# Leaving the sums of two spectral weight products to the inverse transform's matmuls

## The chip, the cores and the metric

The kernel runs on one core of one Trainium2 chip. The metric is the device time of one execution in microseconds (us), given as the median over several runs. A difference under 2% gets the verdict "same", so the 95% interval of each ratio is given too.

## The reference

Two equal layers are applied to a sequence of 2048 rows of 448 elements in bf16. Each is a spectral layer (normalise, two-dimensional real FFT, multiply by a complex weight, inverse FFT, add) followed by a dense layer (normalise, matmul to 1792, squared relu, matmul back, add).

```python
def _A_ref(x, w_r, w_i):
    X = jnp.fft.rfft2(x.astype(jnp.float32), axes=(-2, -1))
    X = X * (w_r + 1j * w_i)
    return jnp.fft.irfft2(X, s=(S, D), axes=(-2, -1)).astype(jnp.bfloat16)

def _B_ref(x, w1, b1, w2, b2):
    h = jnp.einsum("bsd,df->bsf", x, w1) + b1
    h = jnp.where(h > 0, h, 0) ** 2
    return jnp.einsum("bsf,fd->bsd", h, w2) + b2

x = A_x
for _ in range(2):                      # written out twice in the reference
    x = x + _A_ref(_layernorm(x), A_w_r, A_w_i)
    x = x + _B_ref(_layernorm(x), B_w1, B_b1, B_w2, B_b2)
```

What matters is `X * W`. A complex product is four real products, one sum and one difference: Re = Xr·Wr − Xi·Wi, Im = Xr·Wi + Xi·Wr.

## The kernel before

The spectral stage works through nine groups of frequencies, numbered 0 to 8. Seven of them are pairs (p = 2, 3 up to 14, 15). Each group passes through these units: TD (forward transform along the rows, matmuls on TQ), an eviction, B (forward transform along the sequence, matmuls on G), an eviction, W (the products with the weights, on VectorE, into `tmp`), Ws (their sum and difference, on VectorE, into `Z`, which lies in the buffer called `arena`), Bi (inverse transform along the sequence, matmuls whose moving operand is the table H and whose stationary operand comes from `Z`), and an eviction into `VT`. The stage TI then transforms back along the rows.

```python
GROUPS = ((1,), (2, 3), (4, 5), (6, 7), (8, 9), (10, 11), (12, 13), (14, 15), (0,))

def stage_W(ps_, slot):
    ...
    for f, W in enumerate((Wa, Wb)):              # products with w_r, then with w_i
        ...
        tt(... T[:, f], X, a, ALU.mult)           # T is a part of tmp
    if p == 0:
        return
    z = z.rearrange("p q f l -> p f q l")
    rank("Ws")
    for i, op in enumerate((ALU.add, ALU.subtract)):   # the sums
        tt(z[:, 2 * i:2 * i + 2], T[:, :, :, 0], T[:, :, ::-1, 1], op)

def stage_Bi(p, slot):
    ...
    for lb in range(2):
        ...
        plan = [(o(0, None), 2, h(0)), (o(1, None), 0, h(64)), (o(0, None), 3, h(192)), (o(1, None), 1, h(256))]
        for n, (out_, i, w) in enumerate(plan):    # 8 matmuls for one p
            mm(out_, Z[:, slot, i, lb:2 * P:2], w, ...)   # 128 columns, step 2
    evac(VT[...], ps[...], "Bie")
```

A list scheduler within the kernel orders all these units on the engines. Its inputs are the tables PR (a priority for each unit) and EN (which engine may take each eviction). Where TensorE would otherwise be idle, the scheduler inserts "fillers": matmuls of 512 columns on a tile of ones whose result nobody reads, meant to keep the engine's activity up:

```python
def warm_mm(b):
    return lambda e: e.matmul(ps[:, b, :], ones[:], ones[:, None, :].to_broadcast([P, 4, P]), start=True, stop=True)
```

The dense layer that follows needs its input transposed. For some of the rows a transposing DMA does this (`yT<-xin`), and the matmuls on `yT` wait for its landing.

## Time and profile before

| | |
|---|---|
| time before (3 runs) | 265.75 us (265.22 to 265.8) |
| span of the profiled run | 264.1 us |
| stage that changes | 142.82 to 164.35 us (21.53 us) |

Here are three lines of the kernel before: from its page, the busy time of each engine (us, share of the span, number of instructions) and the chain that ended last, by engine; and from busy time by stretch, exactly the stage that changes (length, then PE, PEld, DVE, ACT, POOL, each with its count, then granted clock, DMA share and GB/s):

```profile
PE 255.7 (97%) x2383; PEld 163.3 (62%) x2383; DVE 204.3 (77%) x708; ACT 183.8 (70%) x391; POOL 9.5 (4%) x21
PE 82%; DVE 7%; ACT 7%; DMA 2%; issue 1%; POOL 0%; POOLq 0%; DVEq 0%
142.82:164.35 21.53, 20.50 (x270) 17.42 (x271) 19.97 (x38) 19.23 (x30) 0.00 (x0) 1.00 0.01 2
```

PE is TensorE, PEld its weight loads, DVE VectorE and ACT ScalarE. In the stage three engines are nearly full at once.

### The profile page before, as it was taken

The page shows a single profiled execution, that of the slowest core. Times are in us where ns is not written, and L with a number is a line of the kernel's source. Part 1 is how long each engine was busy: PE and PEld are TensorE (multiplying, and loading weights), DVE is VectorE, ACT ScalarE, POOL GpSimd, SP SyncE. Part 2 cuts the span into 40 slices and gives each one's busy share as a digit, 9 for nine tenths or more (in the row PEclk, how much of TensorE's full clock was granted, in tenths as well). Part 3 has the DMA queues.
Part 4 walks back from the last instruction along what each step waited for, and adds up shares of the span by engine and source line. Part 5 has one row for each costly group of instructions (what it writes and reads, how often), then busy time and mean ns, then how long its engine had stood idle before and what let it go on. Part 6 is the DMA issues. An engine that isn't in the chain of part 4 may idle for free.

```text
span 264.1 us, 6399 instructions
## 1 busy us (share of the span) xinstructions
PE 255.7 (97%) x2383; PEld 163.3 (62%) x2383; DVE 204.3 (77%) x708; ACT 183.8 (70%) x391; POOL 9.5 (4%) x21
## 2 busy tenths in 40 slices
PE   8999999999999999999999999998999999999996
PEld 2679978768555554445577887786754444544454
DVE  4978997999999996565797998899899755223522
ACT  6978996978786388791587996976999784005700
POOL 4720000000000000000000000000000000000000
PEclk9999999999999999999999999999999999999999
DMA  6999990026606700013000000002077000110011
GB/s 185 406 351 359 387 351 21 2 43 132 183 15 151 193 9 2 0 27 116 0 2 0 2 4 0 4 0 60 2 125 149 20 0 20 37 52 19 0 37 52
DMA packets 24474, 23.25 MB, mean 88 GB/s; under 512 B 16284, under 2 KB 20988, under 8 KB 24316
## 3 DMA queue, kind: packets, MB, share of 16 engines
q1 hardware_dynamic: 23968, 21.82, 27.9%
q0 software_dynamic: 160, 0.92, 0.8%
q8 instruction: 19, 0.31, 0.5%
q10 hardware_dynamic: 316, 0.10, 0.2%
q14 instruction: 11, 0.09, 0.1%
HBM read 15.49 MB, written 2.76 MB: 69 GB/s over the span
## 4 chain that ended last, share of the span: by engine, by line
PE 82%; DVE 7%; ACT 7%; DMA 2%; issue 1%; POOL 0%; POOLq 0%; DVEq 0%
PE ps L588 79%; ACT arena L628 3%; PE ps L1157 2%; DVE arena L646 2%; DMA yT<-xin 2%; ACT XA L628 2%; ACT tmp L628 1%; DVE tmp L646 1%; DVE x_raw L936 1%; DVE st L966 1%; ACT VT L628 1%; DVE tmp L629 0%; DVE x_raw L938 0%; DVE VT L646 0%; ACT mv L611 0%
## 5 line engine op out<-in xcount | busy, mean ns | idle before, releaser
L611 ACT ACTIVATE arena<-ps,b1T 128x512 bf16<-128x512 f32 (+1 forms) x140 | 74.0, 614 | 31.2 <-PE ps L588 31.0
L588 PE MATMUL ps<-yT,W_sb 64*128 64x512 bf16 (+1 forms) x980 | 87.1, 333 | 1.1 <-DMA yT<-xin 0.7
L588 PE MATMUL ps<-W_sb,arena 128*128 128x448 bf16 (+1 forms) x476 | 86.8, 342 | 0.0
L588 PEld LDWEIGHTS ps<-yT,W_sb 64*128 64x128 bf16 x980 | 50.3, 94 | 37.4 <-ACT arena L611 5.1
L588 PEld LDWEIGHTS ps<-W_sb,arena 128*128 128x128 bf16 x476 | 46.1, 98 | 37.8 <-DVE arena L646 0.8
L646 DVE TENSOR_TENSOR arena<-arena 128x512 bf16<-128x512 bf16 (+1 forms) x140 | 48.0, 370 | 19.1 <-ACT arena L611 18.7
L1055 DVE TENSOR_TENSOR x_raw<-ps,arena 128x448 bf16<-128x448 f32 (+1 forms) x23 | 13.4, 581 | 20.8 <-PE ps L588 20.8
L628 ACT ACTIVATE arena<-ps 128x896 bf16<-128x896 f32 (+1 forms) x32 | 26.3, 911 | 2.6 <-PE ps L588 2.6
L628 ACT ACTIVATE VT<-ps 128x512 bf16<-128x512 f32 x28 | 16.5, 699 | 2.8 <-PE ps L588 2.7
L1157 PE MATMUL ps<-ones 128*128 128x512 bf16 x54 | 16.4, 428 | 1.1 <-DVE ones L659 1.1
L588 PE MATMUL ps<-H_sb,arena 128*128 128x128 bf16 x256 | 16.8, 219 | 0.7 <-DVE arena L646 0.7
L646 DVE TENSOR_TENSOR arena<-tmp 128x896 bf16<-128x896 bf16 (+1 forms) x32 | 17.1, 590 | 0.3
L738 ACT ACTIVATE tmp<-x_raw 128x448 bf16<-128x448 bf16 x14 | 8.1, 576 | 13.3 <-DVE x_raw L1051 13.2
L628 ACT ACTIVATE XA<-ps 128x512 bf16<-128x512 f32 x28 | 15.2, 593 | 2.4 <-PE ps L588 2.4
L738 ACT ACTIVATE VT<-x_raw 128x448 bf16<-128x448 bf16 x24 | 13.8, 583 | 4.3 <-DVE x_raw L938 4.3
L588 PEld LDWEIGHTS ps<-H_sb,arena 128*128 128x128 bf16 x256 | 15.0, 98 | 2.7 <-DVE arena L646 2.5
L646 DVE TENSOR_TENSOR tmp<-VT 128x224 bf16<-128x224 bf16 (+1 forms) x56 | 16.3, 322 | 0.2
L938 DVE SCALAR_TENSOR_TENSOR x_raw<-ps,x_raw 128x448 bf16<-128x448 f32 x24 | 14.3, 621 | 0.8 <-PE ps L588 0.8
L588 PE MATMUL ps<-arena,G_sb 128*128 128x224 bf16 x128 | 14.4, 259 | 0.1
L628 ACT ACTIVATE tmp<-ps 128x896 bf16<-128x896 f32 (+1 forms) x16 | 12.7, 853 | 1.9 <-PE ps L588 1.9
L758 DVE BATCH_NORM_STATS2 st<-x_raw 128x6 f32<-128x448 bf16 (+1 forms) x19 | 10.9, 589 | 2.5 <-DMA x_raw<-in_A_x_dram 2.5
L588 PEld LDWEIGHTS ps<-arena,G_sb 128*128 128x128 bf16 x128 | 11.8, 98 | 0.7 <-ACT arena L628 0.6
(78 smaller groups left out, 263.5 us busy)
## 6 DMA issues: line engine op xcount, KB each, us to landing
W_sb<-in_B_w_dram SPq DMA_DIRECT2D x2, 896.0 KB, 12.3
out_dram<-x_raw SPq DMA_DIRECT2D x15, 112.0 KB, 1.7
W_sb<-in_B_w_dram SPq DMA_DIRECT2D x1, 1568.0 KB, 17.5
x_raw<-in_A_x_dram SPq DMA_DIRECT2D x3, 448.0 KB, 7.9
H_sb<-c_H SPq DMA_DIRECT2D x1, 1088.0 KB, 9.5
yT<-xin SPq DMA_DIRECT2D x4, 225.0 KB, 5.7
Wrev<-xin SPq DMA_DIRECT2D x2, 450.0 KB
xin<-Wrev SPq DMA_DIRECT2D x4, 225.0 KB, 3.7
```

The source lines that it names most:

```text
L588: op = sch.add("pe", lambda e: e.matmul(_res(o), lhsT, rhs, start=start, stop=stop, skip_group_check=skip), [lhsT, rhs, *also], [o], cost= ...
L611: sch.add("act", lambda e: e.activation(o, _res(i), func, **kw), rd, [o], cost=c)
L628: op = sch.add("act", lambda e: e.activation(o, _res(i), ACT.Copy) if h[0].eng == "act" else e.tensor_copy(o, _res(i)), [i], [o], cost=c[" ...
L646: sch.add(eng, lambda e: e.tensor_tensor(o, _res(a), b, op), [a, b], [o], cost=_free(o) / rate + 69.0)
L738: sch.add("act", lambda e: e.activation(o, x, ACT.Square, accum_out=sd[:, t, 1:2]), [x], [o, sd[:, t, 1:2]], cost=560.0)
L758: small(lambda e, si=si, xi=xi: e.bn_stats(si, xi), [xi], [si], _free(xi) / 0.96 + 69.0)
L936: sch.add("dve", lambda e, xx=xx, xi=xi, r=r: e.tensor_tensor(xx, _res(r), xi, ALU.add), [r, xi], [xx], cost=536.0)
L938: small(lambda e, xx=xx, xi=xi, r=r, i=i: e.scalar_tensor_tensor(out=xx, in0=_res(r), scalar=1.0, in1=xi, op0=ALU.mult, op1=ALU.add, accum ...
L966: small(lambda e, i=i: e.bn_stats(st[:, i, 0:6], x_sb[:, i, 0:D]), [x_sb[:, i, 0:D]], [st[:, i, 0:6]], 536.0)
L1055: sch.add("dve", lambda e: e.tensor_tensor(o, _res(i), xb[:, t, d0:d1], ALU.add), [i, xb[:, t, d0:d1]], [o], cost=(d1 - d0) / 0.96 + 69.0)
L1157: return lambda e: e.matmul(ps[:, b, :], ones[:], ones[:, None, :].to_broadcast([P, 4, P]), start=True, stop=True)
```

## The change

The intent is to take VectorE's sums out of the stage in which VectorE is full. For groups 5 and 7 of layer 2 the inverse matmuls read the products in `tmp` directly and add them up in the accumulator. Because an accumulator only adds, the differences need a negated copy of two blocks of H, which is appended to the table. That makes 16 matmuls for each p in place of 8.

```diff
+DIRECT = ((), (10, 14))
+HX = sorted({q for d in DIRECT for p in d for q in (p, p + 1)})
 ...
-PR = {...}
-EN = {...}
+PR = {...}    # new numbers for layer 2's TD, B, W, Bi, TDe, Be, Ws, Bie; nothing else differs
+EN = {...}    # new choices for layer 2's TDe, Be, Bie
 ...
-        H_sb = sb("H_sb", [P, 15 * HQ + 4 * P])
+        H_sb = sb("H_sb", [P, 15 * HQ + (4 + 2 * len(HX)) * P])
 ...  # make_constants: the negated tables
+                if p in HX:
+                    o = 15 * HQ + (4 + 2 * HX.index(p)) * P
+                    H[:, o:o + P] = -H[:, HQ * (p - 1):HQ * (p - 1) + P]
+                    H[:, o + P:o + 2 * P] = -H[:, HQ * (p - 1) + 192:HQ * (p - 1) + 192 + P]
 ...  # stage_W
-            if p == 0:
+            if p == 0 or direct:
                 return
 ...  # stage_Bi
+                if direct:
+                    x = 15 * HQ + (4 + 2 * HX.index(p)) * P
+                    neg = [H_sb[:, x + f * P:x + (f + 1) * P] for f in range(2)]
+                    plan = []
+                    for f in range(2):
+                        a = tmp[:, 2 * (slot // 2) + f, slot % 2, 0, lb::2]
+                        c = tmp[:, 2 * (slot // 2) + f, mate % 2, 1, lb::2]
+                        plan += [(o(0, None), a, h(192 * f)), (o(1, None), a, h(192 * f + 64)),
+                                 (o(0, None), c, neg[f]), (o(1, None), c, h(192 * f + 64))]
-                    mm(out_, Z[:, slot, i, lb:2 * P:2], w, ...)
+                    mm(out_, i if direct else Z[:, slot, i, lb:2 * P:2], w, ...)
+            m = QD if direct else P       # QD = 112: only 112 partitions are evicted
```

More of the change, by code (lines that the diff above doesn't have):

```diff
@@ L79, in make_constants @@
     G = np.zeros((P, NP + 1, 192))
-    H = np.zeros((P, 15 * HQ + 4 * P))
+    H = np.zeros((P, 15 * HQ + (4 + 2 * len(HX)) * P))
     for p in range(NP):
@@ L111, in make_constants @@
                 J=np.eye(P)[::-1])
-PR = {'TD': [[1611015, 1560745, 1571669, 1391435, 1398832, -3621416, 1374866, -3479716, 1402951], [2520683, -882130, 2513278, 1403817, -946609, -1006157, -1079382, -1083072, 1408461]], 'B': [[1578993, 1416687, 1553212, 1417621, 1401279, -3584572, -3471848, 1550869, -3659354], [2513805, -1004943, 1405526, 2514030, 1385417, -1091018, 967616, -1128168, -974908]], 'W': [[1833706, 1883605, 1713507, 1845799, 1846051, 1858785, 1847117, 1976414, 992154], [258958, 196705, -32086, -31831, 199273, -68617, -58145, -231565, -289839]], 'Bi': [[-3600236, -3636088, 1397759, -3650383, -3634765, -3649053, -3658753, -3646144, -3576979], [-1103789, 969189, -981009, 1254540, 970491, 1105225, 1552262, 1255862, 1105109]], 'ln': [[991126, 1016681, 13698, -12192, 3592, -9275, 58717, 59319, 60173], [-215928, -161644, -233516, -1278285, -1243220, -1249248, -1270637, -1075997, -1090994]], 'TI': [[4661211, 3603451, 3461865, -3320802, 3581733, -3314912, 3577378, -3303437, -3557233], [1148985, 1261825, -1055731, -1010406, -1074609, -1083367, -1026469, -1043258, -1050048]], 'AI': [[3603697, 4997207, 4997530, 4979074, 3482668, 4986081, 4943161, 4901552, 4992029], [-1080862, 1269571, 943460, -1102619, 1036527, 1203915, -1142225, 1214879, 1183541]], 'xb': [[966, 109389, -75965, -110358, -218149, -39133, -137679, -133462, -146632], [-874934, -227306, -1248899, -1550879, -1543334, -1550645, -1548009, -1575947, -1598280]], 'h': [[4994138, 5003910, 4900585, 4903100, 4901125, 4954442, 5002645], [-1085930, 1201108, 1202903, 1171062, 1082119, 1231856, 1056057]], 'o': [[5025464, 5043598, 4946662, 4825629, 4947511, 4769147, 4931712, 4939797, 4905816, 4965852, 4907640, 4758088, 4928290, 3664542, 4936102, 3571000], [1035960, 1041613, 1046935, 1054242, 1080488, 1155787, 1169102, 1155870, 1000585, 1239792, 1159813, 1159789, 1170072, 1159974, 1163403, 1047019]], 'A2': [[-34871, -450185, -573944, -145705, 153605, 80879, -602905, 81580, 79768, -84049, 81902, 81224, 99503, 452346, 464311, 452106]], 'A1': [[2017417, 2016753, 2017368, 2018568, 2015776, 2016320, 2011733, 2013388]], 'aux': [[1784077, 2030436, 1458000, -222125]], 'A1x': [[-78438, 1764055, 2017145, 1740521, 1945455, 2017149, 1733606, 2013750]], 'A1f': [[2026475, 2022846, 1700588, 1673326, 1885756, 2013682, 1843661, 1757672]], 'A1m': [[1624402, 1624407, 1618344, 1618039, 1618053, 1537576, 1602322, 1670734]], 'A1e': [[2018288, 1743124, 2013324, 2018938, 1792872, 2007452, 926476, 1834891]], 'A2f': [[-34049, -127990, -606838, -439476, -138011, 89305, -571804, 80322, 86631, 80269, 450792, 462862, 54580, 466206, 59337, 450170]], 'A2s': [[480058, 130187, 326278, 591247, -431528, 73495, -83424, -22736, -590315, -851545, -746374, -585928, -115865, -441429, 129400, 466571]], 'A2m': [[4922555, 4746350, 4716000, 4727107, 4938752, 4935914, 4721112, 4719912, 3545281, -1102588, 3449906, 3544553, -1101765, 4721131, 3545586, -1101726]], 'A2e': [[43630, 40194, -682618, -204383, 162475, -55941, 457346, -202207, 210383, 251692, -640306, -43305, -207937, 110571, 278833, 493288]], 'TDe': [[2015312, 1881608, 1834874, 1912279, 933173, 1914329, 1811666, 1807467, 2012655], [234287, 1417255, 495995, 497071, -692296, -708408, 116793, 481473, -31496]], 'Be': [[1810378, 2015630, 1839426, 1797362, 938200, 1031040, 933515, 1076416, 1026320], [-673471, -562228, -700927, 509333, -668554, 482845, -571588, -638456, -610624]], 'Ws': [[1843817, 1846443, 1875937, 2003156, 1836055, 1861290, 2004506, 1857296, 1821747], [212971, -52164, -46639, -245211, -58995, -232137, -245502, -184844, -32998]], 'Bie': [[1820631, 1817640, 1818170, 1921951, 1076577, 1873067, 1921957, 1027958, 1022790], [1425225, 487576, -647465, -980124, -655085, -74395, -74265, -181695, -980116]], 'TIe': [[913909, 919877, 722393, -268012, 716509, -288603, 853646, 1008636, 792915], [-149289, -168051, -87569, -1092127, -1364282, -1052619, -148265, -1019412, -75009]], 'AIf': [[-308433, 3579, -182406, 12653, 80551, 7729, -143107, -148725, -142263], [-1045428, -423729, -1430802, -276728, -1103758, -1170272, -918535, -1355679, -1095738]], 'AIs': [[1037824, 921138, 43475, 988, 25617, -29947, -110980, 57417, 53976], [-160854, -145123, -793906, -883581, -1371555, -217899, -1046764, -1245627, -1325531]], 'lnq': [[254432, -546412, 123603, 7472, -193124, -186442, 9410, 836140, -149412], [-287651, -1394001, -1546005, -1125253, -1199492, -1202077, -101648, -1538229, -1522243]], 'lny': [[168910, 899305, 37852, 73400, -12667, 102790, 55869, -23759, 84279], [-244523, -464919, -208553, -1628453, -1450315, -1200119, -1077933, -1545496, -1133605]], 'fl': [[4991518, -3553909, 5045833, 5074410, 3443910, -3419830, 4794596, -3248326, 4963895], [-1100203, -1109390, -1282316, -1178605, -1592271, -1453810, 732254, -1093079, -1088719]], 'fle': [[-189687, 766990, -622264, 878315, -707948, 922239, -284319, -762173, -301700], [-1435726, -776655, -779325, -884711, -359745, -150713, -909732, -337434, -263372]], 'hA': [[-173623, -61538, 82981, 166072, -461795, 94451, 17384], [-59738, -1239374, -1219139, -169082, -1225583, -1223164, -59731]], 'hD': [[24938, -128082, -607193, -606364, -517680, 4299, -81566], [-949150, -1571960, -1533320, -1506174, -1592396, -1567483, -1293058]], 'oD': [[6213, -23599, -603373, -443574, 151235, 130944, 83824, 118459, -119914, 133726, 132035, -4922, 78773, 479772, 77491, 442182], [-1549288, -1077336, -1522386, -1421216, -1499943, -906811, -859800, -1465910, -1534119, -1026687, -1633193, -1551677, -1535519, -1571610, -1461819, -1620002]]}
@@ L116 @@
-EN = {'lny': ['addbdbadb', 'aadbdadbb'], 'A1x': ['bbxqpxda'], 'A1f': ['drxxprdq'], 'A1e': ['baaaaaad'], 'A2s': ['dbbabbabadbbbddb'], 'A2e': ['abaabababdaadbaa'], 'TDe': ['ddabaabaa', 'abadaaaad'], 'Be': ['aabbaabbb', 'abaaabaaa'], 'Bie': ['bbabadaaa', 'aaaaabbda'], 'TIe': ['adbbbbaaa', 'aabdabbbb'], 'fle': ['badababdb', 'bddaabaab']}
+PR = {'TD': [[1611015, 1560745, 1571669, 1391435, 1398832, -3621416, 1374866, -3479716, 1402951], [3344602, -810569, 3542993, -1113711, -1021573, -1404706, -1163469, -1118054, -1018261]], 'B': [[1578993, 1416687, 1553212, 1417621, 1401279, -3584572, -3471848, 1550869, -3659354], [3544915, -1103941, -1021324, -1165847, -1126479, -1162876, -1242708, -1251169, -1161448]], 'W': [[1833706, 1883605, 1713507, 1845799, 1846051, 1858785, 1847117, 1976414, 992154], [242406, 231998, -98658, 363900, 217632, 174073, -101948, 237541, -101711]], 'Bi': [[-3600236, -3636088, 1397759, -3650383, -3634765, -3649053, -3658753, -3646144, -3576979], [-1118253, -1132280, -1251596, -1185249, -1238569, -1179627, -1180641, -1238399, -1178436]], 'ln': [[991126, 1016681, 13698, -12192, 3592, -9275, 58717, 59319, 60173], [-215928, -161644, -233516, -1278285, -1243220, -1249248, -1270637, -1075997, -1090994]], 'TI': [[4661211, 3603451, 3461865, -3320802, 3581733, -3314912, 3577378, -3303437, -3557233], [1148985, 1261825, -1055731, -1010406, -1074609, -1083367, -1026469, -1043258, -1050048]], 'AI': [[3603697, 4997207, 4997530, 4979074, 3482668, 4986081, 4943161, 4901552, 4992029], [-1080862, 1269571, 943460, -1102619, 1036527, 1203915, -1142225, 1214879, 1183541]], 'xb': [[966, 109389, -75965, -110358, -218149, -39133, -137679, -133462, -146632], [-874934, -227306, -1248899, -1550879, -1543334, -1550645, -1548009, -1575947, -1598280]], 'h': [[4994138, 5003910, 4900585, 4903100, 4901125, 4954442, 5002645], [-1085930, 1201108, 1202903, 1171062, 1082119, 1231856, 1056057]], 'o': [[5025464, 5043598, 4946662, 4825629, 4947511, 4769147, 4931712, 4939797, 4905816, 4965852, 4907640, 4758088, 4928290, 3664542, 4936102, 3571000], [1035960, 1041613, 1046935, 1054242, 1080488, 1155787, 1169102, 1155870, 1000585, 1239792, 1159813, 1159789, 1170072, 1159974, 1163403, 1047019]], 'A2': [[-34871, -450185, -573944, -145705, 153605, 80879, -602905, 81580, 79768, -84049, 81902, 81224, 99503, 452346, 464311, 452106]], 'A1': [[2017417, 2016753, 2017368, 2018568, 2015776, 2016320, 2011733, 2013388]], 'aux': [[1784077, 2030436, 1458000, -222125]], 'A1x': [[-78438, 1764055, 2017145, 1740521, 1945455, 2017149, 1733606, 2013750]], 'A1f': [[2026475, 2022846, 1700588, 1673326, 1885756, 2013682, 1843661, 1757672]], 'A1m': [[1624402, 1624407, 1618344, 1618039, 1618053, 1537576, 1602322, 1670734]], 'A1e': [[2018288, 1743124, 2013324, 2018938, 1792872, 2007452, 926476, 1834891]], 'A2f': [[-34049, -127990, -606838, -439476, -138011, 89305, -571804, 80322, 86631, 80269, 450792, 462862, 54580, 466206, 59337, 450170]], 'A2s': [[480058, 130187, 326278, 591247, -431528, 73495, -83424, -22736, -590315, -851545, -746374, -585928, -115865, -441429, 129400, 466571]], 'A2m': [[4922555, 4746350, 4716000, 4727107, 4938752, 4935914, 4721112, 4719912, 3545281, -1102588, 3449906, 3544553, -1101765, 4721131, 3545586, -1101726]], 'A2e': [[43630, 40194, -682618, -204383, 162475, -55941, 457346, -202207, 210383, 251692, -640306, -43305, -207937, 110571, 278833, 493288]], 'TDe': [[2015312, 1881608, 1834874, 1912279, 933173, 1914329, 1811666, 1807467, 2012655], [358792, 137068, 517649, 212723, 370833, 276697, 429087, -1203399, 465388]], 'Be': [[1810378, 2015630, 1839426, 1797362, 938200, 1031040, 933515, 1076416, 1026320], [515039, 320885, -963694, 219491, -950249, 307014, 592380, 552522, 351214]], 'Ws': [[1843817, 1846443, 1875937, 2003156, 1836055, 1861290, 2004506, 1857296, 1821747], [235002, 1304989, 302402, 335116, -138539, 340820, -137935, -1087450, 44319]], 'Bie': [[1820631, 1817640, 1818170, 1921951, 1076577, 1873067, 1921957, 1027958, 1022790], [-1224585, -1347858, -1190193, -1155379, -1284822, -1191842, -1187647, -1203314, -1213324]], 'TIe': [[913909, 919877, 722393, -268012, 716509, -288603, 853646, 1008636, 792915], [-149289, -168051, -87569, -1092127, -1364282, -1052619, -148265, -1019412, -75009]], 'AIf': [[-308433, 3579, -182406, 12653, 80551, 7729, -143107, -148725, -142263], [-1045428, -423729, -1430802, -276728, -1103758, -1170272, -918535, -1355679, -1095738]], 'AIs': [[1037824, 921138, 43475, 988, 25617, -29947, -110980, 57417, 53976], [-160854, -145123, -793906, -883581, -1371555, -217899, -1046764, -1245627, -1325531]], 'lnq': [[254432, -546412, 123603, 7472, -193124, -186442, 9410, 836140, -149412], [-287651, -1394001, -1546005, -1125253, -1199492, -1202077, -101648, -1538229, -1522243]], 'lny': [[168910, 899305, 37852, 73400, -12667, 102790, 55869, -23759, 84279], [-244523, -464919, -208553, -1628453, -1450315, -1200119, -1077933, -1545496, -1133605]], 'fl': [[4991518, -3553909, 5045833, 5074410, 3443910, -3419830, 4794596, -3248326, 4963895], [-1100203, -1109390, -1282316, -1178605, -1592271, -1453810, 732254, -1093079, -1088719]], 'fle': [[-189687, 766990, -622264, 878315, -707948, 922239, -284319, -762173, -301700], [-1435726, -776655, -779325, -884711, -359745, -150713, -909732, -337434, -263372]], 'hA': [[-173623, -61538, 82981, 166072, -461795, 94451, 17384], [-59738, -1239374, -1219139, -169082, -1225583, -1223164, -59731]], 'hD': [[24938, -128082, -607193, -606364, -517680, 4299, -81566], [-949150, -1571960, -1533320, -1506174, -1592396, -1567483, -1293058]], 'oD': [[6213, -23599, -603373, -443574, 151235, 130944, 83824, 118459, -119914, 133726, 132035, -4922, 78773, 479772, 77491, 442182], [-1549288, -1077336, -1522386, -1421216, -1499943, -906811, -859800, -1465910, -1534119, -1026687, -1633193, -1551677, -1535519, -1571610, -1461819, -1620002]]}
@@ L117 @@
+EN = {'lny': ['addbdbadb', 'aadbdadbb'], 'A1x': ['bbxqpxda'], 'A1f': ['drxxprdq'], 'A1e': ['baaaaaad'], 'A2s': ['dbbabbabadbbbddb'], 'A2e': ['abaabababdaadbaa'], 'TDe': ['ddabaabaa', 'daaadabbb'], 'Be': ['aabbaabbb', 'aaabbbbab'], 'Bie': ['bbabadaaa', 'babbaadbb'], 'TIe': ['adbbbbaaa', 'aabdabbbb'], 'fle': ['badababdb', 'bddaabaab']}
 ENG = {"a": ("act",), "d": ("dve",), "p": ("pool",), "b": ("act", "dve"), "q": ("act", "pool"), "r": ("dve", "pool"),
@@ L710, in bass_interleave_layers__spectral_gfnet__dense_activation_squared_relu__prompt_kernel @@
         for n, (p0, p1) in enumerate(RANGES):
-            g1, h1 = (p1 - 1, HQ * (p1 - 1)) if n == 0 else (NP + 1, 15 * HQ + 4 * P)
+            g1, h1 = (p1 - 1, HQ * (p1 - 1)) if n == 0 else (NP + 1, 15 * HQ + (4 + 2 * len(HX)) * P)
             dma("sp", G_sb[:, p0 - 1:g1], dc["G"][:, p0 - 1:g1])
@@ L837, in stage_B, with stage_W @@
             evac(EF[:, p:p + n, :], q[lambda b: ps[:, b:b + n, 0:2 * LW]], "Be")
-        def stage_W(ps_, slot):
+        def stage_W(ps_, slot, direct):
             p, n = ps_[0], len(ps_)
@@ L855, in stage_W, with stage_Bi @@
                 tt(z[:, 2 * i:2 * i + 2], T[:, :, :, 0], T[:, :, ::-1, 1], op)
-        def stage_Bi(p, slot):
+        def stage_Bi(p, slot, direct, mate):
             rank("Bi")
@@ L863, in o @@
                 def o(k, c):
-                    v = lambda b, lb=lb: ps[:, b, 256 * lb:256 * (lb + 1)]
+                    v = lambda b, lb=lb: ps[0:QD if direct else P, b, 256 * lb:256 * (lb + 1)]
                     if c is None:
@@ L871, in h @@
                     return H_sb[:, a:a + P]
-                if p == 0:
+                if direct:
[7 more added lines that the diff above has]
+                                 (o(0, None), c, neg[f]), (o(1, None), c, h(192 * f + 64))]
+                elif p == 0:
                     plan = [(o(None, n % 2), n, h(n * P)) for n in range(4)]
@@ L877, in stage_Bi @@
                 for n, (out_, i, w) in enumerate(plan):
-                    mm(out_, Z[:, slot, i, lb:2 * P:2], w, lb == 0 and n == 0, lb == 1 and n == len(plan) - 1, skip=True)
-            evac(VT[:, :, :, :, 2 * p:2 * p + 2, :].rearrange("p r g t c j -> p (r g) t (c j)"),
-                 q[lambda b: ps[:, b, :].rearrange("p (a t e) -> p a t e", a=4, t=16)], "Bie")
+                    mm(out_, i if direct else Z[:, slot, i, lb:2 * P:2], w, lb == 0 and n == 0, lb == 1 and n == len(plan) - 1, skip=True)
+            m = QD if direct else P
+            evac(VT[0:m, :, :, :, 2 * p:2 * p + 2, :].rearrange("p r g t c j -> p (r g) t (c j)"),
+                 q[lambda b: ps[0:m, b, :].rearrange("p (a t e) -> p a t e", a=4, t=16)], "Bie")
         def stage_TI(t, n, late):
@@ L1084, in spectral @@
                 rank("W", L, n)
-                stage_W(ps_, slot)
+                direct = ps_[0] in DIRECT[L]
+                stage_W(ps_, slot, direct)
                 rank("Bi", L, n)
                 for i, p in enumerate(ps_):
-                    stage_Bi(p, slot + i)
+                    stage_Bi(p, slot + i, direct, slot + len(ps_) - 1 - i)
                 if first and n == 3:
```

## The prediction

> **What bounds the kernel now.** I first read the page's busy table (TensorE busy 97% of 264.1 us, but a matmul's recorded duration overlaps its neighbour's, so this is no proof of a bound), then the chain of work that ended last, to see which engine ends each stage, then busy time by stretch, and last the instructions in order of time in the only stretch that the change touches. That stretch is the second layer's spectral stage, from the first TQ matmul at 142.82 us to the first TI matmul at 164.35 us, 21.5 us in all. The chain there:
>
> ```profile
> 156.73 2.23 DVE arena L646 x5
> 158.96 0.36 issue
> 159.32 1.17 DVE tmp L646 x2
> 160.50 0.03 DVEq L1171
> 160.53 0.50 DVE arena L646
> 161.03 0.05 issue
> 161.07 1.07 PE ps L588 x16
> 162.14 0.00 issue
> 162.15 1.53 PE ps L588 x24
> 163.68 0.02 issue
> 163.70 0.61 ACT VT L628
> 164.30 0.05 issue
> 164.35 1.35 PE ps L588 x17
> ```
>
> Columns: start us, us, what. VectorE's products (tmp) and sums (arena, line 646) set when the last inverse matmuls may start; one eviction by ScalarE (VT) follows, and then the next stage. The order of time says the same of the engines: VectorE runs from 143.81 to 164.1 us without a pause, while TensorE has room that it fills with matmuls on ones that compute nothing:
>
> ```profile
> 156.65 2.76 DVE L646 TENSOR_TENSOR arena<-tmp 128x896 bf16<-128x896 bf16 x5
> ...
> 154.22 1.95 PE L588 MATMUL ps<-H_sb,arena 128*128 128x128 bf16 x32
> 156.00 0.93 PE L588 MATMUL ps<-arena,G_sb 128*128 128x224 bf16 x8
> 156.77 1.46 PE L1157 MATMUL ps<-ones 128*128 128x512 bf16 x6
> ```
>
> ```profile
> 143.00:166.00 23.00, 21.98 (x295) 18.89 (x293) 20.25 (x39) 20.21 (x32) 0.00 (x0) 1.00 0.01 2
> ```
>
> The last line is busy time by stretch: length, then PE, PEld, DVE, ACT, POOL, clock, DMA. VectorE and ScalarE have nearly the same work (20.25 and 20.21 us of 23), the clock is full, and DMA is idle. The reader is to see that an engine relieved here has another close behind it. After 166 us come the inverse transforms, normalisation and the dense layers, none of which changes; from 182 us TensorE streams dense matmuls to the end. So what the stage gains or loses should reach the end almost one for one.
>
> **What the Trainium skill says.**
> 1. "VectorE: DVE Perf Modes", "Side-by-side: where the cycles go for N=2048 bf16": two-tensor operations on 16-bit data go at two elements a cycle at best. Agrees: 896 elements at two per 0.96 GHz cycle are 467 ns; the trace spaces five of them by (2.76 - 0.62)/4 = 0.535 us, fixed cost included.
> 2. "TensorE: Matmul & The Clock Gate", "Back-to-back issue gap": N/2.4 + 2.5 ns, 55.8 ns for N = 128. Agrees: 32 H matmuls took 1.95 us; less one 0.219 us duration that is 1.73/31 = 55.8 ns.
> 3. The same page, "LDWEIGHTS (loading the stationary operand)": a load takes columns/1.2 ns, which would be 107 ns for 128 columns. The trace differs: each of those 32 matmuls has its own load, at 55.8 ns, and the TQ matmuls, 112 wide with a 128-column load each, come every (1.34 - 0.213)/23 = 49.0 ns. So a 128-column load here takes at most 49 ns.
> 4. The same page, "Weight-path perf modes — Fast Weight Load (FWL) and DoubleRow": a fast load is switched on automatically when the number of weights is 128 and the type is not FP32. This fits point 3. I find that every stationary operand of the kernel before has exactly 128 columns, some padded to that with zeros. No run so far shows a load of fewer columns.
>
> **The change part by part.** Groups are numbered as in the kernel, 0 to 8; the changed ones are 5 (p = 10, 11) and 7 (p = 14, 15).
> *Removed from VectorE:* each of the two groups loses its add and its subtract of 896 elements: 4 x 0.535 = 2.14 us, all in the saturated stretch. By the order of instructions one 448-element eviction also moves from ScalarE to VectorE (+0.54 us there, -0.44 on ScalarE). Net VectorE: -1.6 us.
> *Added to TensorE:* the four p of the two groups have 16 matmuls each in place of 8: +32, at 55.8 ns +1.79 us. Gone are 12 of the 14 fillers on ones in the stage (about 0.215 us each, from the timeline's 1.46 us for six; 2.6 us), which stood in gaps.
> *New in kind:* all 64 matmuls of these groups take the products straight from tmp, as 112 columns with step 2, not as 128 padded ones from arena. If point 4 holds, they lose the fast load; by point 3 a load is then 112/1.2 = 93 ns (an estimate from the skill's page), and as every matmul has its own, their spacing is 93 rather than 56 ns.
> *Moved:* all priorities of layer 2's spectral stage are new. In the changed order there is one run of 120 inverse matmuls with nothing between: 16 of group 3, the 64 direct ones, 32 of groups 4 and 6, and 8 of group 8; then the TI stage.
> *Table load:* the second H transfer grows from 1088 to 1344 KB. The one of before lands 9.5 us after its issue at 18.9 us, at 28.4 us; the first matmul that needs it is at 33.3 us. At the 376 GB/s of that stretch 256 KB are 0.7 us, so it still arrives 4 us early: no effect.
>
> Now I lay the new order out by hand, with the durations of before. TensorE starts at 142.82 as before. VectorE starts at 143.6 with three evictions (0.54 + 0.54 + 1.02) and is then free at 145.8; group 0 (4 x 0.31) to 147.0; then 13 operations of 0.535 us, the products of 1, 2, 3 and half of 4 and the sums of 1, 2, 3, to 154.0. ScalarE starts at 143.4, waits once for TensorE near 145.7, and then has ten evictions of 896 at 0.81, one of 448 at 0.44 and one of VT at 0.49 us before group 6's is out: 145.7 + 9.0 = 154.8. That frees the bank for the run of 120, which starts at 154.85.
> Group 5's products are ready at 155.6 and group 7's at 157.2 (ScalarE delivers its input at 156.1), each before its turn in the run. The last sums (4, 6) and products (8) are done at 160.5, also before their turn. So in this last part TensorE is the bound, a turn from before, where VectorE was.
> - Loads at full speed: 120 x 55.8 ns = 6.7 us, to 161.55; the last result 0.2 us later, one VT eviction with its waits 0.6: TI starts at 162.35, 2.0 us earlier than at 164.35.
> - Slow loads: 64 x (93.3 - 55.8) = 2.4 us more on the same path: TI starts at 164.75, 0.4 us later than before.
> Hand layouts forget hand-over times (the chain shows 0.02 to 0.36 us at each change of engine) and I add 0.3 us. So -1.7 us and +0.7 us: 265.75 becomes 264.05 or 266.45.
>
> **The rivals.**
> A. *The adds simply come off VectorE, and TensorE has room for the 32 matmuls.* For it: 14 fillers and the 2.14 us. It makes 264.0. Against it: 112 columns where all others have 128.
> B. *The direct matmuls run at the speed of their weight loads.* For it: points 3 and 4, and that the kernel pays zero padding elsewhere to keep 128 columns. Against it: the skill gives no measured spacing for 112 columns, and if the array loads a column per 2.4 GHz cycle, 47 ns hide under 56. It makes 266.4.
> C. *ScalarE, as loaded as VectorE, becomes the bound.* Its evictions number 29 in place of 30, and from 143.4 us they need about 18.6 us, to 162.0; with waits, the gain falls to 1 us or less: 265.0. Against it: by the layout it has pauses after 157 us, as it had before.
> D. *The fillers' absence lets the clock drop.* The skill's page ("Part 1: The HAM clock gate (the \"warmup\" mystery)") wants an idle window of about 3.4 us; the largest gap in my layout is under 1 us, and the granted clock of before is 1.00. It makes nothing.
>
> **Range and chances.** I give B 0.6 and A with C 0.4, and put the number near B: 266.0 us. The range runs from A with a little less gain forgotten, 263.7, to B with some more lost at hand-overs, 267.1. Two per cent are 5.3 us, more than twice all that either branch moves; within 2% is 0.96, the rest split evenly, for a state of the schedule that I overlook.
>
> **What would show each step.** VectorE: 24 in place of 28 operations of 896 elements in the stage, still spaced by 0.535 us. TensorE: the 64 matmuls on H_sb and tmp; spacing 93 ns (64 last about 6 us) confirms B, 56 ns (3.6 us) confirms A and refutes the step on the fast load. The run of 120 should start near 154.9 us, with no wait for VectorE in it; a wait for arena there would say that VectorE still is the bound, one for VT that ScalarE is (C). The granted clock should stay at 1.00 (D). The first TI matmul should stand at 164.4 to 165.1 us under B, 162.3 to 162.8 under A, and the rest of the span should shift by the same amount; if the stage moves and the end doesn't, the step "one for one" is wrong. The time before the stage should stay within 0.3 us, else the larger table matters after all.

## The result

| | before | after |
|---|---|---|
| median of 6 runs, same rounds | 265.79 us (265.22 to 265.99) | 263.36 us (263.27 to 263.63) |
| ratio, 95% interval | | 0.9913 (0.99 to 0.9925) |
| span of the profiled run | 264.1 us | 261.5 us |
| stage, first TQ to first TI matmul | 142.82 to 164.35, 21.53 us | 142.74 to 162.49, 19.75 us |

A ratio here and below is the mean time of one kernel's runs over that of the other's in the same rounds, so it isn't quite the ratio of the medians. Executions over 1.5% slower than the fastest of the same kernel are left out of the means. The change saves 2.43 us in the medians. The whole interval lies below 1. The measured time is 0.34 us below the low end of the predicted range.

The same three views of the kernel after (the page's busy line, its chain by engine, and the stage in busy time by stretch), and last the stretch from 143 to 166 us that the prediction shows for the kernel before:

```profile
PE 254.6 (97%) x2403; PEld 164.0 (63%) x2403; DVE 202.5 (77%) x705; ACT 183.0 (70%) x390; POOL 9.5 (4%) x21
PE 88%; ACT 6%; DVE 3%; issue 1%; POOL 0%; POOLq 0%; DVEq 0%
142.74:162.49 19.75, 19.41 (x291) 18.09 (x291) 18.37 (x35) 18.52 (x29) 0.00 (x0) 1.00 0.01 2
143.00:166.00 23.00, 22.66 (x340) 21.33 (x338) 20.51 (x39) 21.25 (x34) 0.00 (x0) 1.00 0.01 3
```

In the stage VectorE's busy time has fallen from 19.97 to 18.37 us, TensorE has 291 matmuls instead of 270, and the stage is 1.78 us shorter. The chain has lost the entry "DMA 2%" altogether, and nothing in the diff's intent has to do with that DMA.

The chain of the kernel after through the stage (start us, us, what), and below it the order of time of TensorE:

```profile
145.66 5.41 ACT arena L634 x7
151.07 0.05 issue
151.12 10.69 PE ps L594 x168
161.81 0.02 issue
161.83 0.61 ACT VT L634
162.44 0.05 issue
162.49 1.35 PE ps L594 x17
```

```profile
154.94 1.05 PE L594 MATMUL ps<-H_sb,arena 128*128 128x128 bf16 x16
155.83 3.74 PE L594 MATMUL ps<-H_sb,tmp 128*112 128x128 bf16 x64
159.40 2.40 PE L594 MATMUL ps<-H_sb,arena 128*128 128x128 bf16 x40
161.63 0.59 PE L1174 MATMUL ps<-ones 128*128 128x512 bf16 x2
162.49 1.73 PE L594 MATMUL ps<-TI_sb,VT 112*128 112x224 bf16 x24 [0.26 <-ACT VT L634]
```

From 151 us on the chain is TensorE alone; in the kernel before VectorE stood in it from 156.73 to 161.03 us. Ahead of that, in a part that the prediction's excerpt leaves out, ScalarE's evictions hold the chain: from 143.22 to 151.74 us before, from 145.66 to 151.07 us now. The 64 direct matmuls come every (3.74 − 0.219)/63 = 55.9 ns: they aren't held up by their weight loads. The rest of the gain lies outside the stage. These are the waits of TensorE for the transposing DMA in the kernel before (us in total, times, longest), then its chain from that DMA on, and the DMA's landing:

```profile
PEld ps L588 <- DMA yT<-xin: 1.1, 1, 1.1
PE ps L588 <- DMA yT<-xin: 0.7, 1, 0.7
```

```profile
177.13 4.80 DMA yT<-xin
181.92 0.05 issue
181.97 2.13 PE ps L588 x35
```

```profile
DMA to landing us min/median/max: 4.8/4.8/4.8
```

In the kernel after no wait of TensorE for this DMA is listed. Its chain runs through that time on TensorE, and the same DMA lands sooner:

```profile
172.69 11.39 PE ps L594 x163
```

```profile
DMA to landing us min/median/max: 3.0/3.0/3.0
```

Why would the same transfer take 4.8 us in one kernel and 3.0 us in the other? The trace's packets show most of it. TensorE's instructions arrive by a DMA queue of their own, in packets of 16,384 bytes, 19 in the whole run (the page's queue table has the queue in both kernels as kind "instruction", 19 packets). One such packet takes about 1 us. Counted from the packet records, in slices of 0.2 us:

```
before: packets of the yT load that start in each slice, and the instruction fetch
178.2   49   178.4  173   178.6  175   178.8  162   179.0  156   179.2  154   179.4  153   179.6   21
179.79 to 180.71   one instruction packet, 16,384 bytes
179.8 to 180.6     no packet of the load
180.6    3   180.8    7   181.0    3      (last end 181.06)

after: the fetch lies at 174.59 to 175.59, before the load
176.4  106   176.6  174   176.8  165   177.0  168   177.2  163   177.4  155   177.6  120   177.8    5
```

In the kernel before, the load's last 13 packets (11 of data and 2 of its 32 closing packets of 4 bytes) come only when the fetch is over, and TensorE waits for them. In the kernel after, the fetch is over before the load begins. The load's packets take 2.76 us before and 1.42 us after, which is 1.3 of the 1.8 us. From the last packet to the landing it is 0.86 us before and 0.45 us after; the records don't say what fills the remaining 0.4 us. The Trainium skill describes these fetches in "Runtime: NRT & Kernel Launch", "Instruction fetch mechanics": each engine's instruction memory is refilled in 16 KiB blocks of 256 instructions, over a DMA queue of its own. The trace agrees about: 2383 matmuls and as many loads are 4766 instructions, with TensorE's other 127 records 4893, or 19.1 blocks of 256, and it shows 19 packets (some matmul records can be missing). The same count says that the queue is TensorE's: `after_back` and `both_p64` below, which have 108 and 76 more matmuls on record than the kernel after, show 20. So the 20 additional matmuls (40 instructions) move every later block boundary to an earlier time. By the fetches of the kernel before (167.12 and 179.79 us, 256 instructions apart) 40 instructions are some 2 us (an estimate); with the 1.9 us that the stage gained this makes 3.9 of the 5.2 us by which the fetch moved. The rest stays open.

The sum of the change is then: the stage begins 0.08 us earlier, takes 1.78 us less, and from the first TI matmul to the end it is 98.96 in place of 99.74 us, 0.78 us less, which is the wait for the DMA. Together these are the 2.64 us between the spans.

### The profile page after: what moved, and what is told of

Same layout as the page of the kernel before. It is cut to its first block, busy times and chain, and to the rows that moved or that the text cites. A ratio compares the mean times of both kernels' runs of the same rounds, so it can differ in the third digit from the quotient of the medians.

```text
span 261.5 us, 6432 instructions
## 1 busy us (share of the span) xinstructions
PE 254.6 (97%) x2403; PEld 164.0 (63%) x2403; DVE 202.5 (77%) x705; ACT 183.0 (70%) x390; POOL 9.5 (4%) x21
## 3 DMA queue, kind: packets, MB, share of 16 engines
HBM read 15.75 MB, written 2.76 MB: 71 GB/s over the span
## 4 chain that ended last, share of the span: by engine, by line
PE 88%; ACT 6%; DVE 3%; issue 1%; POOL 0%; POOLq 0%; DVEq 0%
PE ps L594 86%; PE ps L1174 2%; ACT arena L634 2%; ACT XA L634 2%; ACT tmp L634 1%; DVE arena L652 1%; ACT VT L634 0%; DVE x_raw L952 0%; DVE tmp L635 0%; DVE tmp L652 0%; DVE st L982 0%; ACT mv L617 0%; POOL VT L635 0%; ACT arena L617 0%; POOL Fs L646 0%
## 5 line engine op out<-in xcount | busy, mean ns | idle before, releaser
L652 DVE TENSOR_TENSOR arena<-arena 128x512 bf16<-128x512 bf16 (+1 forms) x140 | 47.9, 366 | 19.1 <-ACT arena L617 18.8
L634 ACT ACTIVATE arena<-ps 128x896 bf16<-128x896 f32 (+1 forms) x31 | 25.5, 910 | 3.0 <-PE ps L594 3.0
L634 ACT ACTIVATE VT<-ps 128x512 bf16<-128x512 f32 (+1 forms) x28 | 15.8, 690 | 1.4 <-PE ps L594 1.3
L594 PE MATMUL ps<-H_sb,arena 128*128 128x128 bf16 x224 | 15.0, 219 | 0.3 <-DVE arena L652 0.2
L652 DVE TENSOR_TENSOR arena<-tmp 128x896 bf16<-128x896 bf16 (+1 forms) x28 | 14.9, 583 | 0.2
L1174 PE MATMUL ps<-ones 128*128 128x512 bf16 x42 | 13.3, 448 | 1.1 <-DVE ones L665 1.1
L594 PEld LDWEIGHTS ps<-H_sb,arena 128*128 128x128 bf16 x224 | 13.2, 98 | 1.6 <-DVE arena L652 0.9
## 6 DMA issues: line engine op xcount, KB each, us to landing
H_sb<-c_H SPq DMA_DIRECT2D x1, 1344.0 KB, 10.2
```

The lines of the kernel that those rows point to most:

```text
L594: op = sch.add("pe", lambda e: e.matmul(_res(o), lhsT, rhs, start=start, stop=stop, skip_group_check=skip), [lhsT, rhs, *also], [o], cost= ...
L634: op = sch.add("act", lambda e: e.activation(o, _res(i), ACT.Copy) if h[0].eng == "act" else e.tensor_copy(o, _res(i)), [i], [o], cost=c[" ...
L652: sch.add(eng, lambda e: e.tensor_tensor(o, _res(a), b, op), [a, b], [o], cost=_free(o) / rate + 69.0)
```

## The experiments

For the stage there were two theories: that the relief of VectorE brings the gain, or that the new order of units alone does. One cost was disputed, the load of 112 columns. For the rest of the gain the theory was the instruction fetch that meets the transposing load; its rival was that the stage's gain simply grows on its way to the end. Ten kernels ran, all with correct results. The table gives nine of them below the kernels before and after; "fetch" is the instruction packet of TensorE nearest to layer 2's first transposed load, "landing" is from the issue of that load to its landing.

| run | median us | ratio (95%) | fetch us | load's packets us | landing us | TensorE's matmuls wait for it |
|---|---|---|---|---|---|---|
| before | 265.79 | 1 | 179.79–180.71 | 178.30–181.06 | 4.8 | 0.7 us |
| after | 263.36 | 0.9913 (0.99–0.9925) | 174.59–175.59 | 176.43–177.85 | 3.0 | no |
| prio_only | 266.08 | 1.001 (0.9994–1.0026) | 180.17–181.10 | 178.65–181.42 | 4.8 | 0.7 us |
| direct_only | 264.67 | 0.9963 (0.995–0.9976) | 175.85–176.94 | 177.74–179.15 | 3.1 | no |
| before_shift | 265.78 | 1.0004 (0.999–1.0017) | 177.15–178.07 | 178.97–180.39 | 3.0 | no, but in layer 1 |
| before_shift2 | 265.25 | 0.9976 (0.9962–0.999) | 176.43–177.70 | 178.45–179.86 | 3.0 | no |
| after_back | 263.57 | 0.9924 (0.9908–0.994) | 176.69–177.65 | 176.54–178.91 | 4.0 | no |
| both_layers | 263.81 | 0.992 (0.9906–0.9934) | 176.40–177.51 | 177.01–178.82 | 3.5 | no, but in layer 1 |
| l1_prio | 263.76 | 0.9918 (0.9904–0.9932) | 176.62–177.96 | 177.20–179.27 | 3.7 | no |
| both_p40 | 262.81 | 0.9897 (0.988–0.9915) | 171.71–172.63 | 176.30–177.72 | 3.0 | no |
| both_p64 | 264.64 | 0.9951 (0.9929–0.9973) | 178.83–179.79 | 177.22–179.80 | 4.8 | yes, in both layers |

Each ratio is against the kernel before in the same rounds, whose median was 265.79, 265.85, 265.86 or 265.99 us. The tenth kernel, `loads`, isn't in the table: it measures a cost by itself, and its time (296.3 us with 512 additional matmuls, a single run) says nothing else.

The traces tell the wait for the load from everything else more sharply than the medians do. From layer 2's first TI matmul to the end all kernels have the same work. This stretch takes 98.95 to 98.99 us in the eight kernels whose matmuls don't wait for the load there, and 99.72 to 99.74 us in the three whose matmuls do (before, prio_only, both_p64). From layer 1's first TI matmul to layer 2's first TQ matmul it is 101.63 to 101.66 us in eight kernels, and 102.34, 102.32 and 102.76 us in before_shift, both_layers and both_p64, whose matmuls wait for a load in layer 1. The waits go back to six loads: one in layer 2 of before and prio_only, one in layer 1 of before_shift and both_layers, one in each layer of both_p64. In each a fetch lies over the end of the load's packets, exactly 2 of its 32 closing packets come after the fetch, and the landing takes 4.8 to 5.0 us. A late landing alone isn't a wait: loads issued at 196.00 us in both_layers and 196.19 us in l1_prio met a fetch and took 4.8 us too, and no matmul waited.

### The new order without the new arithmetic (prio_only)

The edit gives the kernel before the new tables PR and EN; all sums stay on VectorE.

```diff
-PR = {...}; EN = {...}    # of before
+PR = {...}; EN = {...}    # of after
```

> The kernel before with the changed kernel's priorities and eviction choices, all sums still on VectorE. If the gain needs the sums to leave VectorE (my theory), VectorE keeps its 28 operations of 896 elements and stays the bound of the stage: 265.5 to 266.5 us, first TI matmul at 164.2 us or later. If the new order alone brings the gain (rival), 263.5 to 264.2 us and the first TI matmul near 162.5 us.

It took 266.08 us (265.57 to 266.68), and the first TI matmul stood at 164.73 us, 0.38 us later than before; the stage took 22.02 us, 0.49 us longer. The order alone gains nothing.

### The new arithmetic without the new order (direct_only)

The edit gives the kernel after the tables PR and EN of before.

```diff
-PR = {...}; EN = {...}    # of after
+PR = {...}; EN = {...}    # of before
```

> The changed kernel's direct products for groups 5 and 7, with the priorities and eviction choices of before. If each sum taken off VectorE is worth its 0.535 us wherever it stands (rival), the full 1.8 us come: 263.4 to 264.0 us. If the order must be fitted so that the direct matmuls have their turn while VectorE still works (my theory), less than two thirds of it: 264.5 to 265.5 us.

It took 264.67 us. Of its 1.2 us, the stage gives only 0.48 us (142.75 to 163.80 us); there is no wait for the transposing load any more, which is the remainder of 0.7 us. So the direct matmuls need the order that was made for them: alone they are worth 0.5 us in the stage, the order alone loses 0.5 us, and together they give 1.78 us.

### What a load of fewer than 128 columns costs (loads)

At the end of the kernel before, eight blocks of 64 matmuls are appended, each matmul with its own load. The moving operand is 32 columns wide in the first four blocks, so that it can't hide the load, and 128 in the last four; the stationary operand has 128, 112, 96 and 64 columns with step 2.

```diff
+            if ename == "pe":
+                eng.wait_ge(sem[("dve", False)], max(o.ticket or 0 for o in sch.ops["dve"]))
+                for n in (32, 128):
+                    for c in (128, 112, 96, 64):
+                        for k in range(64):
+                            eng.matmul(ps[0:c, 2 * (k % 2), 0:n], H_sb[:, k:k + 2 * c:2], ones[:, 0:n], start=True, stop=True)
```

> The kernel before, followed at its end by eight blocks of 64 matmuls on constants, each with its own weight load at column step 2: moving width 32, then 128, with 128, 112, 96 and 64 stationary columns each. If only 128 columns load fast (the step of my prediction that failed), the 112-column block of width 32 has a spacing of 47 ns or more, against 25 to 35 ns for 128 columns. If a load's cost does not depend on it (rival), all blocks of width 32 have one spacing, under 50 ns. At width 128 both spacings should be 56 ns, as the changed kernel shows. The outputs stay right; the run is longer by 15 to 30 us.

The loads in three windows, as the view of the tile H_sb has them (count, duration in ns as min/median/max, first and last start, form): 128 columns; 112 columns at first; 112 columns later. Under them, in a fence of their own, the same time in busy time by stretch:

```profile
L1193 PEld LDWEIGHTS ps<-ones,H_sb x60: 96/98/99, 262.0 to 263.5; 128*128 128x128 bf16 x60
L1193 PEld LDWEIGHTS ps<-ones,H_sb x25: 130/132/134, 263.6 to 264.9; 128*112 128x112 bf16 x25
L1193 PEld LDWEIGHTS ps<-ones,H_sb x32: 209/212/212, 265.3 to 268.2; 128*112 128x112 bf16 x32
```

```profile
264.00:267.00 3.00, 3.00 (x45) 3.00 (x45) 0.00 (x0) 0.00 (x0) 0.00 (x0) 0.71 0.03 5
267.00:270.00 3.00, 3.00 (x37) 3.00 (x37) 0.00 (x0) 0.00 (x0) 0.00 (x0) 0.50 0.00 0
```

Sixty loads of 128 columns start within 1.5 us, 1.5/59 = 25 ns apart, so such a load takes at most that here. The loads of 112 columns are 53 ns apart at first (1.3/24 by the rounded times shown, 53 ns by the records). At 265.26 us the granted clock falls from 1.00 to 0.50, and from there they are (268.2 − 265.3)/31 = 93 ns apart. At 0.50 the loads of 96 and 64 columns were 80 and 53 ns apart. At 0.50 all three come to 0.83 ns a column; at 1.00 the 112 columns come to 0.47 ns each, a little over half of that. With 128 moving columns and the clock back at 1.00, all of 112, 96 and 64 columns came every 55 to 56 ns. (The block of 128 columns by 128 ran mostly at 0.50, 107 ns apart, and can't be compared; 96 and 64 columns under 32 moving ones were measured at 0.50 alone.) So a load of 112 columns takes at least twice as long as one of 128, as point 4 of the prediction expected, and at full clock it still fits beneath a matmul of 128 columns.

The durations in the changed kernel itself say the same; here are its loads on H_sb, those from `tmp` and those from `arena` in the window of the run of 120:

```profile
L594 PEld LDWEIGHTS ps<-H_sb,tmp x64: 130/131/132, 155.8 to 159.3; 128*112 128x112 bf16 x64
L594 PEld LDWEIGHTS ps<-H_sb,arena x6: 98/98/98, 155.6 to 159.5; 128*128 128x128 bf16 x6
```

A direct load's record is 131 ns long, as in the appended block at full clock, and the padded one's is 98 ns; the spacing of the matmuls is 55.9 ns all the same.

### Moving the fetch with the sums unchanged (before_shift, before_shift2)

If the fetch is what the change removed by chance, the kernel before must gain some 0.7 us from 20 more matmuls that compute nothing. After the scheduling, some fillers are cut into several narrower matmuls of the same total width, 20 more in all. In `before_shift` these are the first 14 fillers of the kernel, in `before_shift2` the six just ahead of the stage (140 to 142 us).

```diff
 ...  # where the scheduler puts in a filler
+                    d.warm = bk[1]
 ...
         sch.schedule()
+        fill = [op for op in sch.ops["pe"] if hasattr(op, "warm")][0:14]      # before_shift2: [32:38]
+        for j, op in enumerate(fill):
+            m = 1 + (20 + len(fill) - 1 - j) // len(fill)
+            cut = [512 * k // m for k in range(m + 1)]
+            def pieces(e, b=op.warm, cut=cut):
+                for u, v in zip(cut, cut[1:]):
+                    r = e.matmul(ps[:, b, u:v], ones[:], ones[:, 0:1].to_broadcast([P, v - u]), start=True, stop=True)
+                return r
+            op.fn = pieces
```

> The kernel before with 20 more TensorE matmuls (40 instructions), made by cutting the first fillers on ones into pieces of the same total width; nothing else differs. If a 16 KB fetch of TensorE's instructions that meets the transposed load at 178 to 181 us held that load up (theory), the fetch comes some us earlier, the load lands in about 3.5 us in place of 4.8, the wait of 0.7 us for it at 182 us goes, and the time is 265.0 to 265.3 us. If the late landing was chance (rival), the time is that of before within 0.2 us.

`before_shift` took 265.78 us and gained nothing in total, which is a miss. In layer 2 the fetch did move out of the way (landing 3.0 us, no wait). But in layer 1 another fetch, at 59.05 to 59.98 us, now met a transposed load there (57.44 to 60.00 us, landing 4.9 us where the kernel before has 3.2). The matmuls waited 0.11 us for this load, and SyncE issued its next transfers only when it had landed (61.22 us in place of 59.52 us), so that a later transposed load of the layer came late too. The order of time of TensorE in that kernel shows the wait for that one in brackets:

```profile
67.05 7.30 PE L589 MATMUL ps<-yT,W_sb 64*128 64x512 bf16 x66 [0.35 <-DMA yT<-xin]
```

From 69 us on it ran 0.71 us behind the kernel before, and layer 2 gave that back. The collision had been moved, not removed. This run alone is inconclusive, so the second one cuts fillers that come after layer 1.

> The kernel before with 20 more TensorE matmuls again, but cut from the six fillers on ones just before layer 2, so that layer 1 runs as before. If the late landing of the transposed load in layer 2 comes from the fetch of TensorE's instructions (theory), the fetch ends before or beside the start of the load's packets, the load lands in 3.0 to 3.5 us, the wait near 182 us goes, no new wait appears in layer 1, and the time is 265.0 to 265.3 us. If the shift by itself is worth nothing (rival), 265.7 to 266.0 us.

`before_shift2` took 265.25 us, with 265.99 us for the kernel before in the same rounds: −0.74 us with every sum still on VectorE. Its fetch was over before the load, the landing was 3.0 us, and the matmuls on `yT` start without a wait at 181.34 us, against 181.97 us before, although the stage began 0.16 us later:

```profile
181.34 4.87 PE L589 MATMUL ps<-yT,W_sb 64*128 64x256 bf16 x86
```

### Bringing the fetch back into the changed kernel (after_back)

The same edit in the kernel after, with 108 more matmuls out of the first 20 fillers, was meant to bring a fetch to the place where the kernel before has it.

> The changed kernel with 108 more TensorE matmuls from cut fillers: with the 20 that it has more than before this makes 128, one full fetch of 256 instructions, so that the fetches stand again as in the kernel before. If the fetch matters (theory), one meets the transposed load at 176 to 178 us, TensorE waits for that load, and the time is 263.8 to 264.2 us. If not (rival), 263.3 to 263.6 us.

It took 263.57 us (263.25 to 264.27), only 0.2 us above the kernel after, so most of the expected loss didn't come. The fetch ran from 176.69 to 177.65 us, in the middle of the load's packets and not over their tail. The landing grew from 3.0 to 4.0 us, but the matmuls on `yT` started at 179.45 us instead of 179.32 us, and 0.10 us of that was there before the stage's end (first TI matmul at 162.59 instead of 162.49 us). A load that lands 1 us late costs almost nothing while there is that much slack before its first reader. The same holds for both_layers and l1_prio in layer 2: landings of 3.5 and 3.7 us, no wait of the matmuls.

### The same trick in layer 1 (both_layers, l1_prio)

To beat both kernels, `both_layers` also makes group 5 of layer 1 direct, with new priorities for layer 1 from a random search on the kernel's own scheduler. `l1_prio` has these priorities without the direct group.

```diff
-DIRECT = ((), (10, 14))
+DIRECT = ((10,), (10, 14))     # both_layers; l1_prio keeps ((), (10, 14))
-PR = {...}; EN = {...}
+PR = {...}; EN = {...}         # new numbers for layer 1's TD, B, W, Bi, TDe, Be, Ws, Bie
```

> The changed kernel with group 5 of layer 1 taken direct too, and new priorities for layer 1's spectral stage. If that stage also ends on VectorE (the chain of before has sums and products there from 35.2 to 37.8 us), 0.5 to 1 us less than the changed kernel: 262.3 to 262.9 us. If layer 1 is held by its loads or by TensorE, no gain: 263.2 to 263.8 us.

> The same new priorities of layer 1 without its direct group: layer 2 as in the changed kernel. If the order of layer 1 makes any gain of the run both_layers, it has the same time; if the direct group does, 263.3 us or more.

Layer 1's stage (first TD to first TI matmul) took 21.99 us in the kernel after, 21.49 us in `both_layers` and 22.40 us in `l1_prio`. In that order the direct group is worth 0.9 us, and against the kernel after 0.5 us. But it also began 0.4 us later in both, so `both_layers` is only 0.1 us ahead of the kernel after at layer 1's first TI matmul (40.99 against 41.09 us). The total was 263.81 us, no different from `l1_prio` in the same rounds and 0.45 us above the kernel after (in other rounds; the intervals overlap). Layer 1's fetch, at 58.88 to 59.81 us, met the transposed load there (57.27 to 59.83 us, landing 4.9 us). TensorE waited 0.12 us for it, and again for a later one that was issued behind it:

```profile
66.84 5.35 PE L594 MATMUL ps<-yT,W_sb 64*128 64x512 bf16 x48 [0.31 <-DMA yT<-xin]
```

### Moving the fetches on purpose (both_p40, both_p64)

If that is the reason, `both_layers` with cut fillers must be fast or slow according to where the fetches fall, with the same arithmetic. `both_p40` has 40 more matmuls (from the first 14 fillers), `both_p64` 64 more (from the first 22); the edit is the one shown above with these numbers.

> The run both_layers with 40 more TensorE matmuls from cut first fillers, to move the instruction fetches. Its trace showed layer 1's spectral stage 0.5 us shorter than the changed kernel's, and a fetch beside layer 1's first transposed load (58.9 to 59.8 us), with waits for that load. If the fetch ate the gain (theory), the waits for the transposed loads go and the time is 262.7 to 263.1 us, below the changed kernel. If something else did, it stays at 263.6 to 263.9 us.

> The same with 64 more matmuls, a further half of a fetch's 128: for the same theory, 262.7 to 263.1 us if no fetch meets a transposed load on the path, 263.4 us or more if one does, and the trace should show which.

`both_p40` took 262.81 us (262.76 to 263.26), with its fetches at 54.35 to 55.45 and 171.71 to 172.63 us, ahead of the first load of each layer. A fetch at 66.38 to 67.30 us does meet a later load of layer 1 (landing 3.8 us), and no matmul waits. This is the lowest median, but that it beats the kernel after isn't shown: the two ran in different rounds, the intervals of their ratios overlap, and the profiled spans are 261.3 and 261.5 us. `both_p64` took 264.64 us (263.44 to 265.07): its fetches, at 64.72 to 65.69 and 178.83 to 179.79 us, met a transposed load in each layer. Its waits:

```profile
PEld ps L595 <- DMA yT<-xin: 2.3, 2, 1.2
PE ps L595 <- DMA yT<-xin: 1.6, 2, 0.9
```

The two kernels do the same arithmetic in the same order and differ by 24 matmuls on ones and by 1.8 us.

## Why the prediction was wrong

**The number.** 266.0 us was predicted and 263.36 us measured, below the range. Two steps failed: the term of 2.4 us for slow loads ("New in kind", branch B), which measured nothing, and "one for one", which left out 0.8 us gained after the stage. By the prediction's own steps:

- *VectorE's relief* was right: four operations of 896 elements are gone, and the busy time in the stage fell by 19.97 − 18.37 = 1.60 us, as worked out.
- *The layout of the stage* was right. The run of 120 was to start at 154.85 us and did at 154.94. With loads at full speed TI was to start at 162.35 us before an allowance of 0.3 us for hand-overs; it started at 162.49.
- *"New in kind"*: the mechanism was right and the size wrong. As the appended blocks show, loads of 112 columns do take at least twice as long as those of 128. But the 93 ns, the estimate from the page's columns/1.2, hold at half clock only. At full clock a load takes 53 ns, which the matmul of 55.8 ns hides. The term of 64 x 37.5 ns = 2.4 us in branch B was zero. This mis-sized term moved the centre up by some 2 us. The thought that a column might be loaded in each full clock cycle stood in the prediction, as the case against B, and it deserved more weight: the page gives no clock with its formula, and the trace before had no load of fewer than 128 columns to test it on.
- *"What the stage gains or loses should reach the end almost one for one"* failed. By the first TI matmul 1.86 us were gained, at the end 2.43 us in the medians (2.64 in the spans). The stretch after 166 us was called unchanged; but a term was missing in the sum, the fetch of TensorE's instructions, which in the kernel before held up the tail of the transposed load. Without it the result would have been about 265.75 − 1.86 = 263.9 us, within the range; with it, it fell out. The 0.7 us wait for `yT<-xin` was in the profile before and wasn't asked after.
- *Rival A* with its 264.0 us was right for the stage. *Rival C*: ScalarE holds the chain for 5.41 us early in the stage, and TensorE's wait before the run of 120 ends with ScalarE's eviction at 154.8 us, just as in the layout. The layout had counted this, so no further gain was lost to it. *Rival D* was right: the granted clock in the stage is 1.00. *The table load* cost nothing: it landed after 10.2 in place of 9.5 us, and layer 1's first TI matmul stood at 41.09 us against 41.17.

**What is shown and what is argued.** That the new arithmetic and the new order are both needed is shown by prio_only and direct_only. That the position of the fetches is worth 0.7 to 0.8 us in layer 2 is shown by before_shift2, and by both_p40 against both_p64 for both layers. That the fetch holds the last packets because it occupies a resource which they need is an inference from the packets' times. That 2 of 32 closing packets are late each time fits one of the core's 16 DMA engines being held up, but the records don't say which engine moved a packet. The start of a fetch also moves by 1 to 3 us between runs whose TensorE stream up to there is the same (59.17 us in the kernel before and 60.44 us in the kernel after, in layer 1). What sets that is open, as is the wide spread of both_p64. It bears on the medians too: of the 36 runs of the kernel before (without the outlier), 8 took 265.16 to 265.48 us and 28 took 265.73 to 266.18 us. That the fetch missed the load's end in the 8 would fit, but only one run of each kernel has a trace, so it isn't shown.

## What to carry to other kernels

Sums of products can be left to the accumulator when another engine bounds the stage, but they gain little until the order of work is redone for the relieved engine; and a cost that lies under another one (a 53 ns load under a 56 ns matmul) adds nothing, so it has to be compared with what covers it, at the same clock, before it is added to a sum. Before crediting a small gain to the arithmetic, compare the waits for DMA outside the changed stage: adding a few instructions anywhere moves every later instruction fetch of that engine, and a control with as many instructions that compute nothing tells the two apart. When a DMA's landing time differs between two kernels that move the same bytes, look in the packets for an instruction fetch over its tail.

## What the Trainium skill lacked or had wrong

- "TensorE: Matmul & The Clock Gate", "LDWEIGHTS (loading the stationary operand)": columns/1.2 ns is given without a clock. Loads of 112 columns come every 93 ns at a granted clock of 0.50, as the formula has it, but every 53 ns at 1.00.
- The same page, "Weight-path perf modes — Fast Weight Load (FWL) and DoubleRow": the condition of 128 columns and the factor of about 2 agree. What the section lacks is the spacing to reckon with at full clock: 25 ns or less for 128 columns, 53 ns for 112.
- The same page, "Back-to-back issue gap": it gives some 81 ns as the sustained spacing of pairs of load and matmul at 128 moving columns. Here such pairs came every 55.8 ns with 128 columns and every 55.9 ns with 112, so its formula for single matmuls held for pairs too. The prediction had taken the formula and passed over the 81 ns.
- The same page, "Part 1: The HAM clock gate (the "warmup" mystery)": for a fall of the clock it names idle windows and small idle gaps between groups of matmuls. Here the clock fell to 0.50 about 3.3 us after a stream of matmuls of 32 moving columns had begun, with one issued every 25 to 53 ns and none missing; the only gap was 0.49 us ahead of the stream. It was back at 1.00 at 282.33 us, 5.3 us into the blocks of 128 moving columns. This is a single run, and no run varied it.
- "Runtime: NRT & Kernel Launch", "Instruction fetch mechanics": blocks of 256 instructions over a DMA queue agree with the 19 packets of 16,384 bytes. It calls the cost mostly hidden. It lacks that a fetch of about 1 us can delay a data transfer that it meets, here from 3.0 to 4.8 us from issue to landing and by 0.7 us on the path.
